# Seven block products for attention times input weights, for batches 2 to 4

## The chip, the cores and the metric

The kernel runs on one core of a Trainium2 chip. The metric is the time of one execution on the device in microseconds (us): 2050.67 us before the change, the median of three runs (2050.41 to 2054.49).

## The reference, cut to what matters

```python
# q, k, v: (4, 6080, 256); w_in: (256, 2048); w_out: (2048, 256); all fp32
qn = q / (norm(q, axis=1) + 1e-6)
kn = k / (norm(k, axis=1) + 1e-6)
s = kn.transpose(0, 2, 1) @ qn / tau      # 256 x 256 for each batch
a = softmax(s)
x = (v @ a).reshape(24320, 256)
h = x @ w_in
out = relu(h) ** 2 @ w_out
```

The attention matrix of a batch is only 256 x 256. The kernel therefore never forms `x`: it multiplies the attention matrix into the weights (`a @ w_in`, 256 x 2048, once per batch) and applies the result to `v`. These products of attention and input weights are what the change is about.

## The kernel before

**Tiling.** The 6080 tokens of a batch are cut into six chunks (five of 1024, one of 960 tokens), each as two halves of T = 512 (480) columns. The 2048 hidden units are cut into eight blocks j of 2 x 128. A chunk with a block is a quad; there are 24 x 8 = 192. fp32 accuracy comes from splitting every operand into a high and a low fp32r part and adding three matmuls (high x high, high x low, low x high), so one product is three matmuls. A quad's first layer is a 2 x 2 block product in Strassen-Winograd form: seven products (`m1` to `m7`, line 753) of 128 x 128 weights with 128 x T values. The second layer (line 911) is in that form too for groups of four blocks, three of the seven products being put off to the end of a group (`run_later`).

**Batch preparation.** For each batch the scores `k.T q` are summed over 48 token tiles (line 484), the column norms and the softmax follow (`norms`, `spread`, `exps`), then `attnT` turns the 256 x 256 exponentials with four TensorE transposes and splits them into `aT` in the ring `acc`. For each of four weight groups g, `load_win` brings the two parts of that group's input weights (`wins`, kept in DRAM in split form) to two tiles of the ring `hl`; `fold` makes for each half ch of the output rows a bank of 512 columns out of six matmuls (line 638), and ScalarE takes the bank to the tile `us` (ring `kq`) with the softmax denominator as its scale (line 643). `combine` forms from `us` the sums that the seven-product form needs, splits them and stores them as `wsc`, from where every chunk of the batch loads its weights (`load_wt`). For batches 2 to 4 all of this runs in the shade of the quads of the batch before: scores until quad 30 of its 48, the folds from about quad 34 on.

**What sets the order.** Every step is an `Op` with a key (a place counted in quads), engines and a cost; `Plan.order` simulates the queues and rings and writes one fixed program for each engine. Steps that either ScalarE or VectorE can do (`cast`) go to whichever the plan thinks is earlier. All places, leads and biases stand in the table `PLACE`. PSUM has eight banks: two in the ring `h` (used by `m1`, `m6`, `m7`, the put-off products and the folds), one each for `x` and `z`, four for the outputs. Each ring has a fixed number of buffers; `kq`, `hl` and `D` have three. A bank is used by one instruction after another: the first product's result is copied out, and the next product adds to the same bank:

```python
product(key, q, A11, Bn, True)
add(key, moved(T), lambda e: copy(e, get(X, ...), made[Bn][:, :T]), [(Bn, 0)], [(X, 0)])
...
product(key, q, S2, Bn, False)
```

Of the kernel before, what the change touches and what calls it, by code (L numbers as in the profile page):

```python
# [18 lines left out]

P = 128  # L20

PLACE = {'ahead': {'P': 11.46, 'A': 2.414, 'V': 1.621, 'S': 2.799, 'G': 6.535},
 'shy': {'V': 1.107},
 'look': 46.549,
 'push': 8.133,
 'slack': 0.744,
 'bias': {'V': -0.23, 'A': 3.545},
 'groups': ((0, 1, 2, 3), (4, 5, 6, 7)),
 'fewer': ((0, 1, 2, 3), (4, 5)),
 'few': (1, 23),  # L30
 'evac': 1,
 'under': ('M6', 'M7'),
 'banks': ({'M1': 'h', 'M6': 'h', 'M7': 'h'}, {'M1': 'h', 'M6': 'h', 'M7': 'h'}),
# [2 lines left out]
 'every': 3,  # L36
 'presplit': 1,
 'last': {1: 30, 2: 30},
 'open': (-5.462, -3.775, -0.543, -0.836, 0.232, -0.871, 0.095, -0.386, -1.001),
 'lead': 1,  # L40
 'start': (0.625, 0.747, 1.316, 1.529, 1.896, 2.09, -0.025, -2.364, 0.629, 0.76, 1.022),
 'sums': (1.642, 2.237, 7.525, 7.358, 6.02, 6.63, 15.884, 14.947),
 'scores': {1: (-0.941, 0.895, 0.796, 4.28), 2: (2.337, 1.339, -0.115, 0.265, 0.748, 3.485)},
 'folds': {1: (3.995, 4.387, -0.606, 0.751, 1.253, 1.806)},
 'rows': {0: ((4.09, 5.166, 7.785), (8.216, 8.679, 10.297), (-5.367, -2.655, -0.367, -0.681, 0.414, -0.202, -2.003), (1.829, 0.099), (2.213, 0.355)),
# [14 lines left out]


class Op:
# [204 lines left out]
def act(n):  # L267
    return 0.1 + 0.00083 * n
# [3 lines left out]
def tile_channel_attention_relu2_ffn(ctx, tc, kq, vT, tau, w_in, w_out, outT):  # L272
# [11 lines left out]
    HMAX = 512  # L284
    G = 2
    NGK = NT // G
    EARLY = 12
    LEAD = PLACE["lead"]
    GROUPS = PLACE["groups"]
    FEWER = PLACE["fewer"]  # L290
# [54 lines left out]
    def moved(n):  # L345
        return {"A": act(n)}
# [14 lines left out]
    def store(key, out, in_, r, w, size, e="S"):  # L361
        add(key, {e: 0.45 if e == "S" else 1.0},
            lambda e: (nc.sync if e == "S" else nc.gpsimd).dma_start(out=out(), in_=in_()), r, w, size)
# [7 lines left out]
    def dtile(name, shape, tag=None, bufs=None):  # L371
        if name not in dram:
            dram[name] = scratch.tile(shape, F32, name=tag or "_".join(map(str, name)), **({"bufs": bufs} if bufs else {}))
        return dram[name]
# [45 lines left out]
    def decode_w_in(key, g, lead=0.9):  # L420
        Wn = decode(key, "in", g, "sq" if g else "t4", lead)
        win[0, g] = Wn
        if not PLACE["presplit"]:
            store(key, lambda: dtile(("wins", g), [P, 4, GW]), lambda: made[Wn], [(Wn, 0)], [(("wins", g), 0)], 512)

# [82 lines left out]
    def tiny(key, eng, cost, fn, r, w):  # L508
        add(key, {eng: cost}, lambda e: fn(), r, w)
# [107 lines left out]
    def fold_split(key, b, g):  # L617
        W, w = win[b, g], plan.tile("hl", ("wi", b, g))
        split(key, 1024, lambda: made[W].rearrange("p a b -> p (a b)"),
              lambda: get(w, [P, 2, NH, 2 * GW], F32R)[:, 0].rearrange("p d n -> p (d n)"),  # L620
              lambda: get(w, [P, 2, NH, 2 * GW], F32R)[:, 1].rearrange("p d n -> p (d n)"),
              [(W, 0)], [(w, 0)], [(w, 1)])
        for l in range(2) if b == 0 and PLACE["presplit"] else ():
            store(key, lambda l=l: dtile(("wins", g), [P, 2, NH, 2 * GW])[:, l], lambda l=l: made[w][:, l].bitcast(F32),
                  [(w, l)], [(("wins", g), l)], 512)

    def fold(key, b, g, ch, ring="h"):
        aT, w, bank = ("aT", b, "aT"), ("wi", b, g), plan.tile(ring, ("fb", b, g, ch))
        u = ("us", b, g)
        if u not in plan.ring_of:  # L630
            plan.tile("kq" if b or g else "s", u)
        cs = slice(ch * P, (ch + 1) * P)

        def run(e):
            n = 0
            for d in range(NH):
                for l, r in ((0, 0), (0, 1), (1, 0)):
                    nc.tensor.matmul(out=get(bank, [P, HMAX]), lhsT=made[aT][:, l, d, cs], rhs=made[w][:, r, d, :],  # L638
                                     start=n == 0, stop=n == 3 * NH - 1)
                    n += 1  # L640

        add(key, {"P": 1.36}, run, [(aT, 0), (aT, 1), (w, 0), (w, 1)], [(bank, 0)])
        tiny(key, "A", act(512), lambda: nc.scalar.activation(
            out=get(u, [P, 4, GW])[:, ch:4 - ch:3 - 2 * ch], in_=made[bank].rearrange("p (t f) -> p t f", t=2), func=AF.Copy,
            scale=made["den", b][:, ch:ch + 1]), [(bank, 0), (("den", b), 0), (("den", b), 1)], [(u, ch)])

    def combine(key, b, g, step=1.0):

# [406 lines left out]
    def at(u, fn, *args):  # L1055
        events.append((u, len(events), fn, args))
# [35 lines left out]
    for g in range(EARLY):  # L1092
        for t in range(G):
            k = g * G + t
            at(-0.6 + 0.01 * k if k < LEAD else PLACE["start"][9] + PLACE["start"][10] * (k - LEAD) / (2 * EARLY - LEAD),
               lambda key, g=g, t=t, k=k: score_mm(key, tiles0[1, g], t, s1, k == 0, k == EARLY * G - 1))
    at(PLACE["start"][9] + PLACE["start"][10] + 0.02, lambda key: score_out(key, 1, s1))
    at(PLACE["start"][6], lambda key: decode_w_in(key, 1, PLACE["open"][7]))
    at(PLACE["start"][7], load_v, 1)
    at(PLACE["start"][8], fold_split, 0, 1)  # L1100
# [12 lines left out]
    for b in range(1, B):  # L1113
# [16 lines left out]
        at(max(end + MID, u - tune[-4] + 0.01), norms, b)  # L1130
        at(max(end + 1 + MID, u - tune[-4] + 0.02), spread, b)
        at(max(end + 1.6, u + tune[-2] + 0.01, u - tune[-4] + 0.03), lambda key, b=b: exps(key, b, lambda: made["s_acc", b], [(("s_acc", b), 0)]))
        at(max(end + 2 + MID, u + tune[-2] + 0.02, u - tune[-4] + 0.04), attnT, b)
        for g in range(NG):
            tune = PLACE["folds"][max(x for x in PLACE["folds"] if x <= b)]
            u = end + tune[0] + tune[1] * g
            at(u - tune[2], load_win, b, g)
            at(u + tune[3], fold, b, g, 0)
            at(u + tune[4], fold, b, g, 1)
            at(u + tune[5], combine, b, g)  # L1140
    for i, u in enumerate(SUMS):
        at(u, weight_sums, i)
    done = {}
# [39 lines left out]
    for ci in range(len(chunks)):  # L1183
# [15 lines left out]
                at(ends[ci, "M5"] + 0.001, evacuate, ci)  # L1199
            at(both + 0.002, join, ci)  # L1200
        for m in ("M1", "M6", "M5", "M7"):
            at(max(ends.get((ci, "M1"), 0.0) if m == "M1" else both + 0.002,
                   ends.get((ci, HOME["M5"]), 0.0) if m == "M7" else 0.0, ends.get((ci, HOME[m]), 0.0)), close, ci, m)
    for u, _, fn, args in sorted(events, key=lambda x: x[:2]):
        fn(u, *args)
# [31 lines left out]
```

## Time and profile before

| | |
|---|---|
| median of three runs | 2050.67 us |
| the profiled execution | 2051.52 us |
| its span, first to last instruction | 2049.7 us |
| PE (matmul) busy | 2035.3 us, 99% |
| VectorE (DVE) busy | 1977.5 us, 96% |
| ScalarE (ACT) busy | 1772.8 us, 86% |
| granted TensorE clock, mean | 1.000 |

The span is 1.8 us shorter than the execution that it comes from; what lies around it is no part of the trace. "PE" stands for the matmuls and "PEld" for the weight loads, which overlap them. Matmuls are pipelined and their ends are modelled, so a row's duration is longer than the distance between two starts; distances are read from the timeline or the chain. Busy time is a union, so it can't exceed a stretch.

### The profile page before, as it was taken

What the parts mean: (1) busy time and instruction counts of PE and PEld (TensorE: products, weight loads), DVE (VectorE), ACT (ScalarE), POOL (GpSimd) and SP (SyncE); (2) the same over time, 40 slices, a digit from 0 to 9 for tenths busy, and PEclk for the clock granted to TensorE, in tenths of its full rate; (3) what the DMA queues carried; (4) which work ended last, traced back from release to release, by engine and by line L of the source; (5) the groups of instructions that cost most, each with busy time, mean ns of one, the idle gap of its engine ahead of it and who ended that gap; (6) DMA issues with size and microseconds to landing.
All of it is one profiled execution on the core that took longest, in us unless ns stands there. A gap on an engine that the chain in (4) does not pass through costs nothing.

```text
span 2049.7 us, 28360 instructions
## 1 busy us (share of the span) xinstructions
PE 2035.3 (99%) x9356; PEld 1700.9 (83%) x9356; DVE 1977.5 (96%) x2909; ACT 1772.8 (86%) x2656; POOL 119.0 (6%) x137
## 2 busy tenths in 40 slices
PE   8999999999999999999999999999999999999999
PEld 7888788878888888888888888888888888888887
DVE  7899999999999999999999999999999999999997
ACT  6789899988899999988889989889888888788885
POOL 0000001000001000010001010000000000000000
PEclk9999999999999999999999999999999999999999
DMA  9899989879999999987899999998799987878875
GB/s 377 293 324 346 301 285 298 250 231 307 338 301 312 301 292 281 292 252 232 300 327 320 315 296 283 270 290 249 251 316 293 296 262 235 260 244 244 250 231 136
DMA packets 299651, 578.14 MB, mean 282 GB/s; under 512 B 24432, under 2 KB 183920, under 8 KB 299504
## 3 DMA queue, kind: packets, MB, share of 16 engines
q1 hardware_dynamic: 278864, 508.65, 71.4%
q0 software_dynamic: 20640, 67.67, 17.6%
q8 instruction: 75, 1.23, 0.2%
q14 instruction: 72, 0.59, 0.1%
HBM read 438.57 MB, written 69.99 MB: 248 GB/s over the span
## 4 chain that ended last, share of the span: by engine, by line
PE 93%; DVE 3%; DMA 3%; issue 1%; ACT 0%; SPq 0%; DVEq 0%; ACTq 0%
PE o L911 25%; PE h L753 24%; PE h L911 17%; PE z L753 12%; PE x L753 6%; PE x L484 5%; PE h L638 2%; PE o L484 1%; DMA wt<-wsc 1%; DMA kq<-kq 0%; DMA vt<-w_in 0%; DVE D L800 0%; DVE hl L356 0%; DVE g L356 0%; DVE t L356 0%
## 5 line engine op out<-in xcount | busy, mean ns | idle before, releaser
L753 PE MATMUL h<-vt,wt 128*128 128x512 f32 (+1 forms) x2304 | 623.6, 389 | 0.9 <-DMA wt<-wsc 0.4
L753 PEld LDWEIGHTS h<-vt,wt 128*128 128x128 f32 x2304 | 430.7, 188 | 92.7 <-DVE D L800 2.3
L911 PE MATMUL h<-hl,wo 128*128 128x512 f32 (+1 forms) x1620 | 390.0, 388 | 0.6 <-issue 0.6
L911 PE MATMUL o<-g,wo 128*128 128x512 f32 (+1 forms) x1368 | 372.3, 388 | 0.0
L911 PEld LDWEIGHTS h<-hl,wo 128*128 128x128 f32 x1620 | 303.2, 188 | 62.7 <-issue 1.0
L356 DVE TENSOR_TENSOR hl<-D,hl 128x1024 fp32r<-128x1024 f32 (+1 forms) x270 | 325.1, 1211 | 5.0 <-ACT hl L331 4.3
L753 PE MATMUL z<-vt,wt 128*128 128x512 f32 (+1 forms) x1152 | 324.0, 389 | 1.6 <-DVE s L800 1.5
L911 PE MATMUL o<-t,wo 128*128 128x512 f32 (+1 forms) x1080 | 299.7, 388 | 0.6 <-DMA wo<-wos 0.6
L911 PEld LDWEIGHTS o<-g,wo 128*128 128x128 f32 x1368 | 254.8, 188 | 49.5 <-ACT s_acc L331 0.2
L356 DVE TENSOR_TENSOR g<-s,g 128x1024 fp32r<-128x1024 f32 (+1 forms) x204 | 247.0, 1211 | 7.3 <-ACT g L331 6.8
L753 PEld LDWEIGHTS z<-vt,wt 128*128 128x128 f32 x1152 | 213.8, 188 | 45.8 <-DVE s L800 2.4
L911 PEld LDWEIGHTS o<-t,wo 128*128 128x128 f32 x1080 | 202.2, 188 | 41.6 <-DMA wo<-wos 1.0
L335 ACT ACTIVATE D<-D 128x1024 f32<-128x1024 f32 (+1 forms) x180 | 189.7, 1054 | 34.8 <-DVE D L800 34.0
L335 ACT ACTIVATE s<-s 128x1024 f32<-128x1024 f32 (+1 forms) x204 | 215.7, 1058 | 3.7 <-DVE s L800 3.2
L331 ACT CAST hl<-D 128x1024 fp32r<-128x1024 f32 (+1 forms) x197 | 204.5, 1044 | 12.8 <-DVE D L846 8.9
L491 POOL DMA_DIRECT2D D<-D x90 | 83.8, 932 | 1569.5 <-DVE hl L356 1110.7
L331 ACT CAST g<-s 128x1024 fp32r<-128x1024 f32 (+1 forms) x159 | 166.5, 1047 | 7.7 <-PE o L911 6.9
L331 ACT COPY x<-h 128x512 f32<-128x512 f32 (+1 forms) x192 | 110.7, 577 | 61.6 <-PE h L753 59.7
L753 PE MATMUL x<-vt,wt 128*128 128x512 f32 (+1 forms) x576 | 160.9, 387 | 0.0
L341 ACT ACTIVATE s<-z 128x512 f32<-128x512 f32 (+1 forms) x192 | 113.6, 591 | 28.9 <-PE z L753 28.0
L800 DVE CUSTOM_DVE_ANT_0 D<-z,m 128x512 f32<-128x512 f32 (+1 forms) x180 | 122.8, 682 | 4.3 <-PE z L753 3.4
L753 PEld LDWEIGHTS x<-vt,wt 128*128 128x128 f32 x576 | 108.1, 188 | 21.7
(146 smaller groups left out, 2934.4 us busy)
## 6 DMA issues: line engine op xcount, KB each, us to landing
wt<-wsc SPq DMA_DIRECT2D x368, 256.0 KB, 6.0
wo<-wos SPq DMA_DIRECT2D x180, 512.0 KB, 5.9
wt<-wsc SPq DMA_DIRECT2D x184, 384.0 KB, 5.4
wo<-wod_M SPq DMA_DIRECT2D x270, 256.0 KB, 5.4
kq<-kq SPq DMA_DIRECT2D x82, 512.0 KB, 7.5
D<-D POOLq DMA_DIRECT2D x75, 512.0 KB, 7.9
wsc<-wt SPq DMA_DIRECT2D x32, 896.0 KB, 7.4
v<-vT SPq DMA_DIRECT2D x40, 512.0 KB, 6.7
```

The source lines that it names most:

```text
L331: (nc.scalar.copy if e == "A" else nc.vector.tensor_copy)(out=out, in_=in_)
L335: nc.scalar.activation(out=out, in_=in_, func=AF.Square)
L341: nc.scalar.activation(out=out, in_=in_, func=AF.Relu)
L356: add(key, {"V": vec(n)}, lambda e: nc.vector.tensor_sub(out=l(), in0=x(), in1=h()), (*r, *wh), wl)
L484: nc.tensor.matmul(out=s[:, h * C:(h + 1) * C], lhsT=l, rhs=r, start=first and h == 0 and n == 0, stop=last and n == len(terms) - 1, skip_ ...
L491: add(key, {"G": 1.0}, lambda e: nc.gpsimd.dma_start(out=out(), in_=in_(), accum_op=ALU.add), r, w, size)
L638: nc.tensor.matmul(out=get(bank, [P, HMAX]), lhsT=made[aT][:, l, d, cs], rhs=made[w][:, r, d, :], start=n == 0, stop=n == 3 * NH - 1)
L753: nc.tensor.matmul(out=out[:, :N], lhsT=made[w][:, l, i], rhs=made[v][:, r, :N], start=start and n == 0, stop=n == 2, skip_group_check=True)
L800: nc.vector._custom_dve(TENSOR_ADD_SAT, out=x, in0=made[bank][:, :T], in1=made[m][:, :T], s0=BIG, s1=0.0)
L911: nc.tensor.matmul(out=o[:, :T], lhsT=l, rhs=x[:, :T], start=start and k == 0, stop=stop and k == 2, skip_group_check=True)
```

## The change

For batches 2 to 4, `attn7`, `load7` and `fold7` take the place of `attnT`, `load_win` and `fold`. Two weight groups make a pair p. Over a pair, a 256 x 256 matrix times a 256 x 1024 one is done as a 2 x 2 block product in Strassen-Winograd form: seven products of three matmuls instead of eight. The left sums are made in `attn7` (after the softmax denominator has been multiplied in by two ScalarE instructions of 256 columns), the right ones once for all batches in `load_t` and `make_t` and kept in DRAM as `tin`; for them the weights are also stored unsplit as `winr`. Of odd groups only one half of `wins` is stored. `fold7` runs the seven products through four banks of the ring `h`, one after the other: results are copied out to `us`, and copied back into a bank when a later product adds to them; the last two are added by VectorE. `combine` is as before. `PLACE` has new numbers nearly everywhere, so the whole order of the program is another one. Cut, the diff is:

```diff
@@ -19,15 +19,19 @@
-PLACE = {'ahead': {'P': 11.46, 'A': 2.414, 'V': 1.621, 'S': 2.799, 'G': 6.535},
- 'shy': {'V': 1.107},
- 'look': 46.549,
- 'push': 8.133,
- 'slack': 0.744,
- 'bias': {'V': -0.23, 'A': 3.545},
+PLACE = {'ahead': {'P': 9.551, 'A': 2.463, 'V': 1.607, 'S': 2.935, 'G': 7.569},
+ 'shy': {'V': 5.013},
+ 'look': 52.025,
+ 'push': 8.038,
+ 'slack': 0.738,
+ 'bias': {'V': -0.132, 'A': 3.725},
+ 'early': 12,
+ 'seven': 1,
+ 'tm': (27.56, 31.697, 3.095, 1.083),
+ 'f7': {1: (1.757, 2.079, 2.342, 2.691, 3.159, 7.39, 1.336)},
...
@@ -36,27 +40,31 @@
- 'lead': 1,
- 'scores': {1: (-0.941, 0.895, 0.796, 4.28), 2: (2.337, 1.339, -0.115, 0.265, 0.748, 3.485)},
- 'folds': {1: (3.995, 4.387, -0.606, 0.751, 1.253, 1.806)},
+ 'lead': 3,
+ 'scores': {1: (0.247, 0.392, 0.673, 0.976), 2: (2.672, 1.326, -0.168, 0.534, 0.738, 5.009)},
+ 'folds': {1: (4.022, 4.398, 5.291, -0.121, -1.916, -3.605)},
...
+        if PLACE["seven"]:
+            store(key, lambda: dtile(("winr", g), [P, 4, GW]), lambda: made[Wn], [(Wn, 0)], [(("winr", g), 0)], 512)
         if not PLACE["presplit"]:
...
+        lo = g % 2 if PLACE["seven"] else 0
         for l in range(2) if b == 0 and PLACE["presplit"] else ():
-            store(key, lambda l=l: dtile(("wins", g), [P, 2, NH, 2 * GW])[:, l], lambda l=l: made[w][:, l].bitcast(F32),
-                  [(w, l)], [(("wins", g), l)], 512)
+            store(key, lambda l=l: dtile(("wins", g), [P, 2, NH, 2 * GW])[:, l, lo:], lambda l=l: made[w][:, l, lo:].bitcast(F32),
+                  [(w, l)], [(("wins", g), l)], 256 * (2 - lo))
...
+    SEVEN = {"M1": ("A11", (0, 0)), "M2": ("A12", (0, 1)), "M6": ("S2", (1, 0)), "M5": ("S1", (1, 1)), "M3": ("S4", (2, 0)),
+             "M7": ("S3", (2, 1)), "M4": ("A22", (3, 0))}
+    LEFT = {"A12": ("aT", 0), "A22": ("aT", 1), "S1": ("aT", 2), "S2": ("aT", 3), "S3": ("aS", 0), "S4": ("aS", 1), "A11": ("aZ", 0)}
+    def attn7(key, b):
+        bank, S, den, en = plan.tile("h", ("ab", b)), plan.tile("sq", ("as", b)), ("den", b), ("s_acc", b)
+        def exp_of(h):
+            return made[en][:, h * C:(h + 1) * C]
+        for h in range(NH):
+            tiny(key, "A", act(C) + 0.05, lambda h=h: nc.scalar.activation(
+                out=exp_of(h), in_=exp_of(h), func=AF.Copy, scale=made[den][:, h:h + 1]),
+                [(en, 1 + h), (den, 0), (den, 1)], [(en, 1 + h)])
+        def turned():
+            v = get(bank, [P, HMAX]).rearrange("p (d c) -> p d c", d=NH)
+            for h in range(NH):
+                for d in range(NH):
+                    nc.tensor.transpose(out=v[:, d, h * P:(h + 1) * P], in_=exp_of(h)[:, d * P:(d + 1) * P], identity=ident)
+        tiny(key, "P", 0.9, turned, [(en, 1 + h) for h in range(NH)], [(bank, 0)])
+        def x(k):
+            return get(S, [P, 8, P])[:, k]
+        add(key, moved(512), lambda e: copy(e, get(S, [P, 8, P])[:, :4].rearrange("p a b -> p (a b)"), made[bank]),
+            [(bank, 0)], [(S, k) for k in range(4)])
+        for k, fn, a, c in ((4, nc.vector.tensor_add, 1, 3), (5, nc.vector.tensor_sub, 4, 0), (6, nc.vector.tensor_sub, 0, 1),
+                            (7, nc.vector.tensor_sub, 2, 5)):
+            alu(key, P, lambda k=k, fn=fn, a=a, c=c: fn(out=x(k), in0=x(a), in1=x(c)), [(S, a), (S, c)], [(S, k)])
+        for ring, name, lo, hi in (("acc", "aT", 2, 6), ("s_acc", "aS", 6, 8), ("zq", "aZ", 0, 1)):
+            n = plan.tile(ring, (name, b, "7"))
+            split(key, (hi - lo) * P, lambda lo=lo, hi=hi: made[S][:, lo:hi],
+                  lambda n=n, w=hi - lo: get(n, [P, 2, w, P], F32R)[:, 0], lambda n=n, w=hi - lo: get(n, [P, 2, w, P], F32R)[:, 1],
+                  [(S, k) for k in range(lo, hi)], [(n, 0)], [(n, 1)])
+    def load_t(key, p):
+        for g in (2 * p, 2 * p + 1):
+            n = plan.tile("kq", ("tw", g))
+            load(key, lambda n=n: get(n, [P, 4, GW]), lambda g=g: dram["winr", g], [(("winr", g), 0)], [(n, 0), (n, 1)], 512)
+    def make_t(key, p):
+        a, c, S = ("tw", 2 * p), ("tw", 2 * p + 1), plan.tile("sq", ("ts", p))
+        def x(n, d):
+            return get(n, [P, 4, GW])[:, 2 * d:2 * d + 2]
+        for o, i, j in (((S, 0), (c, 1), (c, 0)), ((S, 1), (c, 0), (a, 0)), ((c, 0), (c, 1), (S, 1)), ((c, 1), (a, 1), (c, 0))):
+            alu(key, 512, lambda o=o, i=i, j=j: nc.vector.tensor_sub(out=x(*o), in0=x(*i), in1=x(*j)), [i, j], [o])
+        for n, ts in ((S, ("T3", "T1")), (c, ("T2", "T4"))):
+            t = plan.tile("hl", ("tx", p, ts[0]))
+            split(key, 1024, lambda n=n: made[n].rearrange("p a b -> p (a b)"),
+                  lambda t=t: get(t, [P, 2, NH, 2 * GW], F32R)[:, 0].rearrange("p d n -> p (d n)"),
+                  lambda t=t: get(t, [P, 2, NH, 2 * GW], F32R)[:, 1].rearrange("p d n -> p (d n)"),
+                  [(n, 0), (n, 1)], [(t, 0)], [(t, 1)])
+            for d, name in enumerate(ts):
+                store(key, lambda name=name: dtile(("tin", p, name), [P, 2, 2 * GW]), lambda t=t, d=d: made[t][:, :, d].bitcast(F32),
+                      [(t, 0), (t, 1)], [(("tin", p, name), 0)], 512)
+    def load7(key, b, p, i):
+        n = plan.tile("hl" if i < 3 else "kq", ("w7", b, p, i))
+        if not i:
+            for l in range(2):
+                load(key, lambda l=l: get(n, [P, 2, NH, 2 * GW], F32R)[:, l].bitcast(F32),
+                     lambda l=l: dram["wins", 2 * p][:, l], [(("wins", 2 * p), l)], [(n, l)], 512)
+            return
+        for d, name in enumerate((("T2", "T1"), ("B22", "T3"), ("T4",))[i - 1]):
+            src = ("wins", 2 * p + 1) if name == "B22" else ("tin", p, name)
+            load(key, lambda d=d: get(n, [P, 2, NH if i < 3 else 1, 2 * GW], F32R)[:, :, d].bitcast(F32),
+                 lambda src=src, name=name: dram[src][:, :, 1] if name == "B22" else dram[src],
+                 [(src, 0), (src, 1)] if name == "B22" else [(src, 0)], [(n, d)], 512)
+    def fold7(key, b, p, i):
+        us = [("us", b, 2 * p + t) for t in range(2)]
+        if not i:
+            for n in us:
+                plan.tile("kq", n)
+        bank = plan.tile("h", ("f7", b, p, i))
+        def slot(n, ch):
+            return get(us[n], [P, 4, GW])[:, ch:4 - ch:3 - 2 * ch]
+        def all_of():
+            return get(bank, [P, HMAX]).rearrange("p (t f) -> p t f", t=2)
+        def mm(m, first):
+            left, (part, d) = SEVEN[m]
+            name, k = LEFT[left]
+            a, w = (name, b, "7"), ("w7", b, p, part)
+            def run(e):
+                for n, (l, r) in enumerate(((0, 0), (0, 1), (1, 0))):
+                    nc.tensor.matmul(out=get(bank, [P, HMAX]), lhsT=made[a][:, l, k], rhs=made[w][:, r, d], start=first and n == 0,
+                                     stop=n == 2, skip_group_check=True)
+            add(key, {"P": 0.68}, run, [(a, 0), (a, 1), *([(w, 0), (w, 1)] if not part else [(w, d)]), *(() if first else [(bank, 0)])],
+                [(bank, 0)])
+        def out(n, ch):
+            add(key, moved(512), lambda e: copy(e, slot(n, ch), all_of()), [(bank, 0)], [(us[n], ch)])
+        def back(n, ch):
+            add(key, moved(512), lambda e: copy(e, all_of(), slot(n, ch)), [(us[n], ch)], [(bank, 0)])
+        def plus(n, ch):
+            alu(key, 512, lambda: nc.vector.tensor_add(out=slot(n, ch), in0=all_of(), in1=slot(n, ch)),
+                [(bank, 0), (us[n], ch)], [(us[n], ch)])
+        for fn, *args in (((mm, "M1", True), (out, 1, 0), (mm, "M2", False), (out, 0, 0)),
+                          ((back, 1, 0), (mm, "M6", False), (out, 0, 1)),
+                          ((back, 0, 1), (mm, "M5", False), (out, 1, 1), (mm, "M3", False), (out, 1, 0)),
+                          ((mm, "M7", True), (plus, 1, 1), (mm, "M4", False), (plus, 0, 1)))[i]:
+            fn(*args)
...
-        at(max(end + 2 + MID, u + tune[-2] + 0.02, u - tune[-4] + 0.04), attnT, b)
-        for g in range(NG):
+        at(max(end + 2 + MID, u + tune[-2] + 0.02, u - tune[-4] + 0.04), attn7 if PLACE["seven"] else attnT, b)
+        for p in range(NG // 2) if PLACE["seven"] else ():
+            tune, f7 = PLACE["folds"][max(x for x in PLACE["folds"] if x <= b)], PLACE["f7"][max(x for x in PLACE["f7"] if x <= b)]
+            u = end + tune[0] + 2 * tune[1] * p
+            for i in range(4):
+                at(u + f7[i] - f7[6], load7, b, p, i)
+                at(u + f7[i], fold7, b, p, i)
+            for t in range(2):
+                at(u + f7[4 + t], combine, b, 2 * p + t)
+        for g in range(NG) if not PLACE["seven"] else ():
             tune = PLACE["folds"][max(x for x in PLACE["folds"] if x <= b)]
             u = end + tune[0] + tune[1] * g
             at(u - tune[2], load_win, b, g)
             at(u + tune[3], fold, b, g, 0)
             at(u + tune[4], fold, b, g, 1)
             at(u + tune[5], combine, b, g)
+    for p in range(NG // 2) if PLACE["seven"] else ():
+        at(PLACE["tm"][p], load_t, p)
+        at(PLACE["tm"][p] + PLACE["tm"][2 + p], make_t, p)
     for i, u in enumerate(SUMS):
```

Left out are the new numbers of `PLACE` for the start, the norms, the sums and the rows of single chunks, a few lines at the start that keep two keys in order, and a condition in the order of `close`.

## Rows read from the trace of the kernel before

**Rows 1.** The page's first parts: span, then each engine's busy time, share and instructions.

```profile
span 2049.7 us, 28360 instructions
PE 2035.3 (99%) x9356; PEld 1700.9 (83%) x9356; DVE 1977.5 (96%) x2909; ACT 1772.8 (86%) x2656; POOL 119.0 (6%) x137
```

**Rows 2.** Busy time by stretch (us; the stretch's length stands behind its bounds).

```profile
0.00:60.00 60.00, 53.35 (x240) 45.72 (x241) 45.50 (x59) 37.12 (x44) 0.83 (x7) 1.00 0.99 381
200.00:450.00 250.00, 246.69 (x1146) 202.79 (x1145) 242.57 (x350) 230.69 (x339) 15.46 (x18) 1.00 0.89 275
390.00:600.00 210.00, 208.96 (x941) 173.95 (x940) 203.41 (x321) 185.81 (x288) 10.83 (x11) 1.00 0.88 285
900.00:1110.00 210.00, 209.96 (x961) 176.19 (x960) 206.82 (x327) 183.03 (x285) 11.66 (x12) 1.00 0.89 288
1600.00:2000.00 400.00, 400.00 (x1769) 331.05 (x1768) 386.40 (x556) 334.72 (x502) 17.93 (x21) 1.00 0.82 251
2000.00:2049.70 49.70, 45.75 (x211) 39.15 (x209) 36.09 (x50) 27.84 (x41) 3.16 (x3) 0.98 0.50 132
```

**Rows 3.** PE's waits over the span, three of seven rows.

```profile
PE x L484 <- DMA kq<-kq: 5.4, 2, 3.5
PE z L753 <- DVE s L800: 1.5, 1, 1.5
PE h L753 <- ACT uM L331: 0.3, 1, 0.3
```

**Rows 4.** The chain that ended last: start, length, work; one block product.

```profile
486.82 2.72 PE h L638 x12
```

**Rows 5.** PE's timeline at the first block products of batch 2: start, length.

```profile
441.00 2.88 PE L638 MATMUL h<-hl,acc 128*128 128x512 f32 x12
443.83 3.02 PE L911 MATMUL h<-hl,wo 128*128 128x512 f32 x12
```

**Rows 6.** Groups by shape: busy us, mean ns of one | idle before.

```profile
L638 PE MATMUL h<-hl,acc 128*128 128x512 f32 x186 | 46.8, 390 | 0.0
L638 PEld LDWEIGHTS h<-hl,acc 128*128 128x128 f32 x186 | 34.9, 188 | 7.3
L643 ACT ACTIVATE kq<-h,den 128x512 f32<-128x512 f32 x30 | 20.6, 686 | 8.4 <-PE h L638 8.2
L331 ACT COPY z<-h 128x512 f32<-128x512 f32 x160 | 94.0, 588 | 3.9 <-PE h L753 2.1
L331 ACT COPY h<-uM 128x512 f32<-128x512 f32 x28 | 16.7, 597 | 1.8 <-DVE D L800 1.1 <-DVE uM L1002 0.6
L1002 DVE TENSOR_TENSOR uM<-h,uM 128x512 f32<-128x512 f32 x57 | 39.3, 689 | 3.4 <-PE h L911 3.0
L875 DVE TENSOR_TENSOR sq<-sq 128x128 f32<-128x128 f32 x32 | 7.9, 287 | 0.1
L662 DVE TENSOR_TENSOR sq<-kq 128x256 f32<-128x256 f32 x30 | 12.2, 420 | 1.3 <-ACT kq L643 1.3
L331 ACT CAST hl<-D 128x1024 fp32r<-128x1024 f32 x160 | 168.2, 1054 | 9.7 <-DVE D L846 5.9 <-PE h L911 2.9 <-PE x L484 0.5
L331 DVE CAST hl<-D 128x1024 fp32r<-128x1024 f32 x65 | 44.9, 691 | 0.0
```

**Rows 7.** VectorE's timeline, three instructions on end: start, length.

```profile
436.19 1.23 DVE L356 TENSOR_TENSOR g<-s,g 128x1024 fp32r<-128x1024 f32 x1
437.32 0.69 DVE L846 TENSOR_TENSOR D<-D,s 128x512 f32<-128x512 f32 x1
437.92 0.70 DVE L825 TENSOR_TENSOR D<-D 128x512 f32<-128x512 f32 x1
```

**Rows 8.** Busy time of VectorE's casts and copies alone (line 331), by stretch.

```profile
390.00:600.00 210.00, 10.82 (x20) 1.00 0.88 285
900.00:1110.00 210.00, 14.13 (x27) 1.00 0.89 288
```

**Rows 9.** DMA issues: queue, count, KB each, median us to landing.

```profile
hl<-wins SPq DMA_DIRECT2D x24, 512.0 KB, 7.2
```

More of the change, by code (lines that the diff above doesn't have):

```diff
@@ L38 @@
  'last': {1: 30, 2: 30},
- 'open': (-5.462, -3.775, -0.543, -0.836, 0.232, -0.871, 0.095, -0.386, -1.001),
- 'lead': 1,
- 'start': (0.625, 0.747, 1.316, 1.529, 1.896, 2.09, -0.025, -2.364, 0.629, 0.76, 1.022),
- 'sums': (1.642, 2.237, 7.525, 7.358, 6.02, 6.63, 15.884, 14.947),
- 'scores': {1: (-0.941, 0.895, 0.796, 4.28), 2: (2.337, 1.339, -0.115, 0.265, 0.748, 3.485)},
- 'folds': {1: (3.995, 4.387, -0.606, 0.751, 1.253, 1.806)},
- 'rows': {0: ((4.09, 5.166, 7.785), (8.216, 8.679, 10.297), (-5.367, -2.655, -0.367, -0.681, 0.414, -0.202, -2.003), (1.829, 0.099), (2.213, 0.355)),
[14 rows of a table removed]
+ 'open': (-5.563, -3.638, -0.344, -0.914, 0.355, -0.936, 0.068, -0.148, -0.729),
+ 'lead': 3,
+ 'start': (0.74, 1.133, 1.303, 1.759, 1.78, 1.927, 0.191, -2.295, 0.321, 0.886, 0.989),
+ 'sums': (1.573, 1.142, 4.885, 7.723, 7.067, 7.798, 14.829, 14.467),
+ 'scores': {1: (0.247, 0.392, 0.673, 0.976), 2: (2.672, 1.326, -0.168, 0.534, 0.738, 5.009)},
+ 'folds': {1: (4.022, 4.398, 5.291, -0.121, -1.916, -3.605)},
+ 'rows': {0: ((3.564, 5.166, 7.184), (8.077, 8.65, 10.317), (-5.323, -3.04, -0.305, -1.041, 1.335, 1.133, -2.199), (1.754, 0.836), (1.929, 0.327)),
[18 rows of a table added]
 class Op:
@@ L286, in tile_channel_attention_relu2_ffn @@
     NGK = NT // G
-    EARLY = 12
+    EARLY = PLACE["early"]
     LEAD = PLACE["lead"]
@@ L1094, in tile_channel_attention_relu2_ffn @@
             k = g * G + t
-            at(-0.6 + 0.01 * k if k < LEAD else PLACE["start"][9] + PLACE["start"][10] * (k - LEAD) / (2 * EARLY - LEAD),
+            at(-0.6 + 0.01 * k if k < LEAD else max(PLACE["start"][9] + max(PLACE["start"][10], 0.0) * (k - LEAD) / (2 * EARLY - LEAD), -0.6 + 0.01 * k),
                lambda key, g=g, t=t, k=k: score_mm(key, tiles0[1, g], t, s1, k == 0, k == EARLY * G - 1))
-    at(PLACE["start"][9] + PLACE["start"][10] + 0.02, lambda key: score_out(key, 1, s1))
+    at(PLACE["start"][9] + max(PLACE["start"][10], 0.0) + 0.02, lambda key: score_out(key, 1, s1))
     at(PLACE["start"][6], lambda key: decode_w_in(key, 1, PLACE["open"][7]))
@@ L1201, in tile_channel_attention_relu2_ffn @@
         for m in ("M1", "M6", "M5", "M7"):
-            at(max(ends.get((ci, "M1"), 0.0) if m == "M1" else both + 0.002,
+            at(max(max(ends.get((ci, "M1"), 0.0), ends.get((ci, "M6"), 0.0) + 0.001 if GS[ci] else 0.0) if m == "M1" else both + 0.002,
                    ends.get((ci, HOME["M5"]), 0.0) if m == "M7" else 0.0, ends.get((ci, HOME[m]), 0.0)), close, ci, m)
```

32 rows, old and new, of the table PLACE are left out of this document.

## The prediction

> **What bounds the kernel now.** I first read the engines' shares [rows 1]: PE is busy for 2035.3 of 2049.7 us, VectorE for 1977.5, ScalarE for 1772.8. A busy PE need not be a PE at its pace, so the second view is the pace: in the chain, twelve matmuls of one block product take 2.72 us [rows 4], 0.2267 us for each start, though a matmul's own row says 0.390 us [rows 6]. At that pace a quad of 14 products x 3 matmuls takes 9.5 us. The reader is to see next, in the table of stretches [rows 2], where PE stands: from 1600 to 2000 us it is busy for 400.00 of 400 us, and so it is nearly everywhere; its idle time is 6.65 us in the first 60, 3.3 us from 200 to 450, and 3.95 us after 2000 us, where the last products, copies and stores follow one another. The waits by name [rows 3] say that the start waits for score tiles, and that in all of the span PE waits 0.3 us for a ScalarE copy. So the time is the number of matmuls times their pace, and whatever takes matmuls away in the middle moves the end, as long as VectorE and ScalarE keep up. That is the second thing to see: VectorE is at 98.5% from 900 to 1110 us and at 97.0% from 200 to 450. It is almost a second bound.
>
> **PE.** Before, a pair of weight groups takes 2 groups x 2 halves x 6 = 24 matmuls; after, 7 products x 3 = 21. With 2 pairs in each of three batches that is 6 x 3 = 18 fewer, 18 x 0.2267 = 4.08 us [rows 4]. The turning of the attention matrix stays at four transposes a batch. The lower bound of a matmul's worth is its weight load, 188 ns [rows 6]: 3.4 us; the upper one is its row's 390 ns: 7.0 us. I take 4.1, since the row of the chain is this very instruction back to back.
>
> [...]
>
> **VectorE.** `fold7` adds two sums of 512 columns a pair; a row of the same form is 0.689 us [rows 6], and on end such instructions start 0.60 us apart [rows 7]: 4 a batch, 2.4 to 2.8 us. `attn7` adds four sums of 128 columns at 0.287 us, and its three splits (512, 256, 128 columns in place of one of 512) add a 256 and a 128 subtraction, 0.420 + 0.287 us [rows 6]: 1.9 us. Together 4.3 to 4.6 us a batch. `make_t` runs twice, once for all batches: four subtractions of 512 columns and two of 1024 (1.13 us apart, 1.23 long [rows 7]): 4.7 to 5.2 us each time, 9.3 to 10.4 in all. The whole is 22 to 24 us more, on an engine that has 72 us idle.
>
> **ScalarE.** A pair goes from four scaled copies at 0.686 us to five plain copies out at 0.588 and two back at 0.597 [rows 6]: +1.4 us, 2.8 a batch. `attn7` has two scalings and a bank copy, and up to two more casts, each no longer than a 512-column copy: at most 2.9 us. With four 1024-column casts at 1.054 us for `make_t`, 4.2 us, the whole is at most 3 x 5.7 + 4.2 = 21 us, with 277 us idle.
>
> **Where that goes.** The places in the table of the diff put `make_t` at quads 31 and 33 and batch 2's products from quad 34 on, that is at about 390 to 600 us, as the first block products of batch 2 now run at 441 us [rows 5]. There VectorE has 210 - 203.4 = 6.6 us idle [rows 2], and about 14 us are added. What is over, 7.4 us, has a way out: 10.8 us of casts that VectorE does in that stretch can go to ScalarE [rows 8], where a cast takes 1.054 us for 0.691 [rows 6], so 11.3 us. ScalarE then gets 11.3 + 5.7 + 4.2 = 21 us and has 24.2 idle [rows 2]. It fits, with 3 us left. From 900 to 1110 us (batch 3, without `make_t`) VectorE has 3.2 us and gets up to 4.6, and ScalarE has 27.0 for 5.7 and 2; that fits easily, as for batch 4. So I cost both engines at nothing, and the cover is this: ScalarE's idle time. If it fails in the first stretch, up to 7.4 us show.
>
> **Banks and hand-overs.** Inside a pair PE now waits for a copy or sum five times before it may add to a bank (for both copies back, and before M2, M3 and M4). What is queued behind such a wait on PE is everything, since its order is fixed; so the plan has to put other products between. The same form, product, copy out, next product into the same bank, stands in every quad, and PE loses 0.3 us to copies in the whole run [rows 3]. The block products of now are not free either: the put-off product behind them takes 3.02 us for twelve matmuls instead of 2.72 [rows 5, 4], 0.3 us lost with both banks of the ring full. I take nothing for the 30 hand-overs; bounds are a gain of 3.6 us (0.3 at each of today's 12 groups saved) and an uncovered copy of 0.6 us [rows 6] at each, 18 us. The transposes of `attn7` wait longer too, since the denominators must now be there and multiplied in first; that is once a batch, four short instructions, in the quads between scores and products, and I count it with these bounds.
>
> **DMA.** Kept sums and unsplit weights cost 2 + 2 + 2 MB once and spare 1 MB of `wins`; a pair loads 2.25 MB for 2.0. That is 6.5 MB beside 578, and some 30 more issues on SP's queue; POOL's gets none. They land in about 7.2 us, as the weights of the folds do [rows 9], and the products are asked for 1.3 quads, 12.7 us, after their loads. Cost nothing; behind a late one stand the weights of the next quads on the same queue, and then PE.
>
> **The new order.** Every place in the program moves. The 3.3 us of PE idle from 200 to 450 us [rows 2] belong to waits that a new order meets differently; the bounds are that they go, or come twice. I take 1 us less, an estimate by a third of them. The start and the end (6.65 and 3.95 us) I leave: loads and stores set them.
>
> **The sum.** -4.1 + 0 + 0 + 0 - 1 = -5.1 us. Against the profiled execution (2051.52 us, 1.8 above its span) that is 2046.4; that execution lay 0.85 above the median of the runs, so 2045.6 us against 2050.67.
>
> **The rivals.**
> - *Nothing comes of it:* the first stretch overflows. Behind on VectorE, PE waits for the sums that free its banks. The price is the 7.4 us of overflow at most, about half in a mild case: 2050.67 - 4.1 + 3.7 = 2050.3. For it speak only 3 us of slack in ScalarE over 210; against it, that work can slide by some quads.
> - *Slower: the hand-overs show.* If three of the five in each pair are uncovered, 6 x 3 x 0.6 = 10.8 us come and 4.1 go: 2057.4. It decides from 8.2 us on (1.4 us, some two uncovered copies, a pair). The 0.3 us that PE waits for copies now [rows 3] speaks against it; that VectorE and ScalarE are fuller when a copy is asked for speaks for it.
> - *Faster still:* all 3.3 us of the waits from 200 to 450 us go, and the squeeze of 0.3 us at 12 groups as well: 2050.67 - 4.1 - 3.3 - 3.6 = 2039.7.
> - *The matmuls taken away are worth less than their pace,* 3.4 us by the weight loads [rows 6], as these stay PE's real limit: 2047.3. [...]
>
> **How the numbers follow.** The measurement can't tell less than about 0.2%, 4.1 us, from no change; faster therefore means below 2046.6. Chances: the forecast 45% (2043 to 2048 as its own range, a good two thirds of it below 2046.6), nothing 25%, slower 15%, faster still 12%, the weight-load limit 3%. From these: faster 0.47, same 0.36, slower 0.17. The range goes from the faster case, 2040, to just short of the slower one, 2056.
>
> **What would show it.** Right: matmuls of the block products fall from 144 to 126 in batches 2 to 4; PE busy falls by 4 us with its idle time as before; VectorE busy rises by less than 24 us as casts move to ScalarE, whose busy time rises by 20 to 40. Wrong: new rows in PE's waits named after a copy, a sum in `us` or a load of `tin`; a PE below 208 us busy from 390 to 600; or a time changed mostly before 60 or after 2000 us, which this argument leaves alone.

## The result and the profile after

The changed kernel takes 2067.65 us (median; 2067.2 to 2069.66) beside 2051.64 us for the kernel before on the same chip: a ratio of 1.0078, 95% interval 1.006 to 1.0095. It is 16 us slower, above the range of 2040 to 2056. The first lines of the page of the changed kernel:

```profile
span 2065.9 us, 28506 instructions
PE 2040.4 (99%) x9338; PEld 1696.2 (82%) x9338; DVE 1986.0 (96%) x2921; ACT 1806.1 (87%) x2723; POOL 119.3 (6%) x137
```

The 18 matmuls are gone, 9338 in place of 9356 [rows 1], and yet PE is busy for 5.1 us more and idle for 11.1 us more. The idle time is waiting, and by the rows the longer busy time is too: a matmul's row is 390 ns long where starts lie 227 ns apart [rows 6, 4], so a gap of up to some 160 ns (the difference, an estimate) can count as busy, and the clock stayed at 1.000. The busy time by stretch (PE, PEld, VectorE, ScalarE, GpSimd, each with its number of instructions, as in [rows 2]) tells where:

```profile
200.00:450.00 250.00, 244.91 (x1135) 200.65 (x1134) 245.70 (x359) 229.70 (x340) 15.63 (x18) 1.00 0.95 296
390.00:600.00 210.00, 205.60 (x902) 166.03 (x901) 204.70 (x323) 185.39 (x294) 9.92 (x10) 1.00 0.93 305
900.00:1110.00 210.00, 207.93 (x946) 173.29 (x946) 203.30 (x325) 186.50 (x296) 10.79 (x11) 1.00 0.89 287
1600.00:2000.00 400.00, 400.00 (x1766) 330.73 (x1765) 388.40 (x563) 337.70 (x507) 18.87 (x21) 1.00 0.84 259
```

PE was idle for 1.0 us from 390 to 600 us and for 0.04 from 900 to 1110 [rows 2]; now it is 4.4 and 2.1. The number of matmuls says more than the idle time: from 390 to 600 us it is 902 for 941, 39 fewer, of which the change takes away 6. The other 33 are 7.5 us at 0.2267 us each, an estimate, and more than a third of the 20 us lost (16 us, and the 4.1 us not gained). From 1600 us on, where no batch is prepared, it runs nearly as before, 1766 matmuls for 1769. VectorE and ScalarE are hardly fuller in these stretches, so it isn't one engine that is full. PE's waits by name (total, times, longest) have 22 rows where there were seven [rows 3], most under 1 us and for all sorts of work:

```profile
PE x L494 <- DMA kq<-kq: 4.5, 2, 3.4
PE h L879 <- DMA wt<-wsc: 3.0, 1, 3.0
PE h L1037 <- ACT m L339: 1.5, 2, 0.8
```

One such place, from the timelines of PE, ScalarE and VectorE of the changed kernel:

```profile
518.30 2.90 PE L1037 MATMUL h<-hl,wo 128*128 128x512 f32 x12
521.03 0.85 PE L1037 MATMUL o<-g,wo 128*128 128x480 f32 x3
521.72 0.82 PE L1037 MATMUL o<-t,wo 128*128 128x480 f32 x3
523.04 0.93 PE L879 MATMUL h<-vt,wt 128*128 128x512 f32 x3 [0.50 <-DVE uM L1128]
524.61 0.93 PE L879 MATMUL h<-vt,wt 128*128 128x512 f32 x3 [0.65 <-ACT m L339]
```

```profile
524.00 0.56 ACT L339 COPY m<-h 128x480 f32<-128x480 f32 x1 [2.14 <-PE h L879]
```

```profile
521.27 0.64 DVE L364 TENSOR_TENSOR t<-D,t 128x480 fp32r<-128x480 f32 x1
521.84 0.54 DVE L364 TENSOR_TENSOR wt<-kq,wt 128x384 fp32r<-128x384 f32 x1
522.31 0.67 DVE L1128 TENSOR_TENSOR uM<-h,uM 128x512 f32<-128x512 f32 x1
```

A put-off product (the first row) ends at about 521.2 us; the sum that gives its bank of the ring `h` back stands third in VectorE's order and ends at 522.98. PE has six more matmuls for the output banks and then only products for that ring, so it waits, first for VectorE and then for ScalarE, which stood idle for 2.14 us before its copy. No engine but VectorE is full here (busy for 7.00 us from 518 to 525, ScalarE for 3.70); the three orders just don't meet well. That raises the question of the experiments: is it the new products, or the new order?

### The profile page after: what moved, and what is told of

The parts are those of the page before. It is cut to its first block, busy times and chain, and to the rows that moved or that the text cites. A ratio compares the mean times of both kernels' runs of the same rounds, so it can differ in the third digit from the quotient of the medians.

```text
span 2065.9 us, 28506 instructions
## 1 busy us (share of the span) xinstructions
PE 2040.4 (99%) x9338; PEld 1696.2 (82%) x9338; DVE 1986.0 (96%) x2921; ACT 1806.1 (87%) x2723; POOL 119.3 (6%) x137
## 3 DMA queue, kind: packets, MB, share of 16 engines
q8 instruction: 75, 1.23, 0.2%
## 4 chain that ended last, share of the span: by engine, by line
PE 82%; DVE 9%; ACT 4%; DMA 3%; issue 1%; SPq 0%; DVEq 0%; ACTq 0%
PE o L1037 23%; PE h L879 21%; PE h L1037 15%; PE z L879 11%; PE x L879 5%; PE x L494 4%; DVE hl L364 2%; PE h L751 1%; DVE D L926 1%; DMA kq<-kq 1%; PE o L494 1%; DVE g L364 1%; DVE t L364 1%; DMA wt<-wsc 1%; ACT s L343 1%
## 5 line engine op out<-in xcount | busy, mean ns | idle before, releaser
L951 DVE TENSOR_TENSOR D<-D 128x512 f32<-128x512 f32 (+1 forms) x180 | 121.8, 677 | 5.7 <-ACT D L343 5.6
```

What stands on the lines that cost most here:

```text
L951: alu(key, T, lambda: nc.vector.tensor_sub(out=delta(q, 0), in0=delta(q, 0), in1=delta(q, 1)), [(D, k), (D, k + 1)], [(D, k)])
```

## The experiments

The ratios are to the kernel before, run beside each group.

| run | products, table, edit | us | ratio, 95% interval |
|---|---|---|---|
| e1 | eight, new table | 2074.24 | 1.0112 (1.0097 to 1.0127) |
| e2 | seven, old table | 2092.39 | 1.0201 (1.0185 to 1.0216) |
| e3 | eight, old table, new general numbers | 2061.54 | 1.005 (1.0034 to 1.0067) |
| e4 | eight, old table, one key moved | 2055.56 | 1.0016 (1.0007 to 1.0025) |
| e5 | as changed, sums on GpSimd, order kept | 2078.86 | 1.0131 (1.0116 to 1.0146) |
| e6 | as changed, no copies back, order kept | 2068.38 | 1.0076 (1.0056 to 1.0097) |
| e7 | as changed, less for VectorE, order kept | 2069.11 | 1.0081 (1.0057 to 1.0104) |
| e8 | e6 and e7 together, order kept | 2069.35 | 1.0081 (1.0066 to 1.0096) |
| e9 | eight, old table shaken | 2075.23 | 1.0114 (1.0097 to 1.0131) |
| e10 | seven, old table shaken | 2109.92 | 1.0282 (1.0267 to 1.0297) |
| e11 | eight, new table refitted | 2060.38 | 1.0044 (1.0029 to 1.0059) |
| e12 | seven, old table refitted | 2077.21 | 1.0123 (1.0108 to 1.0138) |
| e13 | seven, old table, ordered without hand-overs | 2076.56 | 1.0125 (1.0106 to 1.0144) |
| e14 | the same, shaken | 2088.67 | 1.0187 (1.0171 to 1.0203) |
| e15 | e13 without the new sums | 2080.45 | 1.0144 (1.0129 to 1.016) |
| e16 | the same, shaken | 2088.64 | 1.0176 (1.0159 to 1.0193) |

**Order against products (e1 to e4).**

```diff
 # e1, to the changed kernel
- 'seven': 1,
+ 'seven': 0,
- 'folds': {1: (4.022, 4.398, 5.291, -0.121, -1.916, -3.605)},
+ 'folds': {1: (3.995, 4.387, -0.606, 0.751, 1.253, 1.806)},
 # e2, to the table of before, with the functions of the changed kernel
+ 'seven': 1,
+ 'tm': (27.56, 31.697, 3.095, 1.083),
+ 'f7': {1: (1.757, 2.079, 2.342, 2.691, 3.159, 7.39, 1.336)},
 # e3, to the kernel before: 'ahead', 'shy', 'look', 'push', 'slack', 'bias' as in the diff
 # e4, to the kernel before
- 'folds': {1: (3.995, 4.387, -0.606, 0.751, 1.253, 1.806)},
+ 'folds': {1: (3.995, 4.387, -0.606, 0.76, 1.253, 1.806)},
```

> New table of places, but the products as they were: eight in place of seven for each pair of groups, no kept sums (the fold keys of before are put back, since the new table has no use for them). If the new order is what costs (theory A), it stays near the changed kernel's 2067 us or lies 4 us above it, 2063 to 2073, and PE again loses some 15 us to waits scattered over the whole span. If the seven products are what costs (theory B: hand-overs between engines inside a pair, and more work for VectorE and ScalarE), it falls back to 2046 to 2054.

> The reverse: the table of places of before, with only the entries that the seven products need taken from the new one. Theory A (order): 4 us fewer matmuls and little else, 2044 to 2052. Theory B (products): 2060 to 2070, with the losses near 390 to 600, 900 to 1110 and 1380 to 1600 us, where the products stand.

> The kernel before with only the general numbers of the plan (how far each engine may run ahead, shyness, look, push, slack, bias) taken from the new table; keys and products are old. Theory A in its narrow form (the general numbers cost): 2060 or more. Theory A in its wide form (any order that was not fitted to this program costs): also above 2051, by 3 us or more. Theory B: 2048 to 2054.

> The kernel before with one fold key moved by 0.009 quads (0.1 us), which gives another order of the program from batch 2 on and changes nothing in the work. It measures what an arbitrary new order is worth. Theory A in its wide form: above 2051.6 by 3 us or more. Theory B, and theory A in the form that only particular places of the new table are bad: within 2 us of the kernel before.

Both theories are half right, and e1 and e2 lie above the ranges of both. The new table with the old products is 22.6 us slower than before, so a new order costs without any of the new work. More than half of it shows from 390 to 600 us, where e1 starts 54 matmuls fewer (887 for 941 [rows 2], some 12 us) and where the fold keys put back from the old table meet the new one:

```profile
390.00:600.00 210.00, 202.10 (x887) 166.40 (x886) 197.68 (x314) 168.43 (x262) 11.19 (x11) 0.98 0.84 266
```

The old table with the new products is slower still, by 40.7 us. A single key moved by 0.1 us costs 3.9 us (ten runs; 1.4 to 5.1 us by the interval), the general numbers alone cost 9.9. The old table is fitted to the old products closely, and each of these changes falls off that fit.

**Load and hand-overs in a fixed order (e5 to e8).** Every engine keeps the order of the changed kernel; the plan is told of the old costs.

```diff
 # e5: attn7's four sums, make_t's four, and make_t's low parts
-nc.vector.tensor_sub(...)
+nc.gpsimd.tensor_sub(...)
 # e6, in fold7
-(back, 1, 0), (mm, "M6", False)
+(mm, "M6", True)
-(back, 0, 1), (mm, "M5", False)
+(mm, "M5", True)
-(mm, "M1", True), (out, 1, 0), (mm, "M2", False)
+(mm, "M1", True), (mm, "M2", False)
 # e7: plus, attn7's and make_t's sums are not emitted; in make_t's splits
-nc.vector.tensor_sub(out=l(), in0=x(), in1=h())
+nc.vector.tensor_copy(out=l(), in_=x())
 # e8: e6 and e7
```

> The changed kernel with every engine's order kept, only that the SBUF sums which the change added (four in the preparation of the attention matrix, all of those for the kept weight sums with their low parts) run on GpSimd, which is idle, in place of VectorE: some 12 us less for VectorE. If the load that the change puts on VectorE is what PE waits for (theory B1), some 4 to 8 us come back, above all from 390 to 530 us: 2059 to 2064. If the waits are laid down in the order itself (theory A), at most 2 us: 2065 to 2069.

> The changed kernel, order kept, without the copy of the first product out and the two copies back into the bank, so that the second and third bank start fresh (the sums of the seven products are then incomplete): 18 ScalarE copies (10.6 us) fewer and two hand-overs a pair in place of five. Theory B2 (the hand-overs inside a pair cost): 5 to 10 us come back, 2057 to 2063. Theory A: less than 2 us, 2065 to 2069.

> The changed kernel with every engine's order kept and most of VectorE's added work left out: the two sums of a pair that end its products, the four sums in the preparation of the attention matrix and the four sums for the kept weights are not done, and the low parts of the latter are plain copies (the result lacks these sums). VectorE has some 16 us less to do, in the stretches where the products stand. Theory B1 (VectorE's added load): 8 us or more come back, 2052 to 2060. Theory A (the order itself): within 3 us of the changed kernel, 2064 to 2070.

> As the run before it, and also without the copy of the first product out and the two copies back, so that VectorE has 16 and ScalarE 10 us less and only one hand-over a pair is left (the result lacks these sums). If load and hand-overs cost only together (theory B), most of the 16 us come back: 2050 to 2058. Theory A: 2062 to 2069.

e6, e7 and e8 are within 2 us of the changed kernel (e8 0.35 us above its range for theory A). The stretch from 390 to 600 us of e7:

```profile
390.00:600.00 210.00, 205.84 (x904) 166.45 (x903) 198.78 (x310) 185.70 (x294) 9.92 (x10) 1.00 0.94 304
```

VectorE has 5.9 us less to do there than in the changed kernel, and PE still does 904 matmuls where it did 902. e6 and e8 say the same, 904 and 898. So neither VectorE's added load nor the inner hand-overs, as they run, are what PE waits for in this order. ScalarE's added work is only in part taken out here, and the added transfers not at all. e5 lies outside both of its ranges: it went the other way, by 11 us. A subtraction of 1024 columns takes 2.78 us on GpSimd, for 1.23 on VectorE [rows 7]:

```profile
L364 POOL TENSOR_TENSOR hl<-kq,hl 128x1024 fp32r<-128x1024 f32 x2 | 5.6, 2782 | 0.9 <-DVE hl L339 0.9
```

These late sums stand ahead of the first block products, so e5 moves a chain as well as a load and tells nothing of the load alone.

**Any order, and a fitted one (e9 to e12).**

```diff
 # e9 (and in the same way e10, on the table of e2): every number shaken
-PLACE = {'ahead': {'P': 11.46, 'A': 2.414, 'V': 1.621, 'S': 2.799, 'G': 6.535},
+PLACE = {'ahead': {'P': 11.436, 'A': 2.422, 'V': 1.641, 'S': 2.789, 'G': 6.508},
 # e12, to e2 (two lines of many; e11 in the same way, to e1)
- 'tm': (27.56, 31.697, 3.095, 1.083),
+ 'tm': (26.007, 30.646, 5.024, 3.473),
- 'f7': {1: (1.757, 2.079, 2.342, 2.691, 3.159, 7.39, 1.336)},
+ 'f7': {1: (1.737, 2.312, 2.362, 3.575, 2.905, 6.345, 1.366)},
```

> The kernel before with every place and number of its table moved a little (normal, 0.02 quads, 0.2 us): the same work, another order throughout. Theory A (an order not fitted to the program costs, whatever the products): 2062 to 2082. Theory B (only the seven products cost): 2049 to 2056.

> The same shaking of the old table with the seven products. If the products ask no more of an order than the eight did, it lies 4 us below the shaken kernel with eight, give or take 10. If they are harder to place (theory A and B together: more steps that lean on one another in the same two banks and three buffers), it lies 25 to 45 us above it: 2095 to 2120.

> Eight products, from the new table, then fitted again: some 2000 small changes of the table, of which those were kept that the plan liked better. Theory A: most of the loss of the unfitted one (2074 us) goes, 2055 to 2065. Theory that the new table's places are bad in themselves: 2070 or more.

> Seven products, from the old table, fitted again with as many changes. Theory A alone: it gets as far as the refitted kernel with eight and lies about 4 us below it, 2051 to 2061. Theory A with harder products: it gains from 2092 but stays 8 us or more above the refitted kernel with eight, 2066 to 2080.

Shaking the table costs the old products 23.9 us. This is one draw, and a good half of it is lost before 200 us, ahead of every product that the change replaces: e9 starts 18 matmuls fewer in the first 60 us (222 for 240 [rows 2]) and 47 fewer from 60 to 200, together some 15 us, with a granted clock of 0.96 in both stretches. The second one, in the kernel before and in e9:

```profile
60.00:200.00 140.00, 140.00 (x621) 115.74 (x620) 129.23 (x212) 120.75 (x188) 1.02 (x1) 1.00 0.90 316
60.00:200.00 140.00, 136.11 (x574) 110.47 (x574) 113.84 (x188) 105.87 (x163) 0.00 (x0) 0.96 0.79 278
```

The seven products lie 34.7 us above the eight when shaken and 16.8 us above them when refitted. These pairs are not orders of like quality, though. e10 shares only the general numbers with e9; its keys are another draw, which loses nothing before 200 us. e11 and e12 were fitted from different tables. And the outputs of e10 and e12 are wrong although their edits leave no work out. In e12 the fitted places put `combine` of a pair's first group (2.905) ahead of the pair's last bank (3.575), so it reads `us` without the last sum; for e10 no run shows what goes wrong. That the fit and the products are two separate costs is what these runs suggest, not what they show.

**What makes the seven products hard to place (e13 to e16).** Here the plan makes a new order for the reduced work.

```diff
 # e13 (old table) and e14 (shaken), in fold7
+(mm, "M1", True), (mm, "M2", False), (out, 0, 0)
+(mm, "M6", True), (out, 0, 1)
+(mm, "M5", True), (mm, "M3", False), (out, 1, 0)
+(mm, "M7", True), (mm, "M4", False), (out, 1, 1)
 # e15 and e16, also: attn7's and make_t's four sums cost nothing in the plan and are not emitted
```

> Seven products in the old table (2092 us), ordered anew without the inner hand-overs: the first product isn't copied out, nothing is copied back, and the last product's sums are left out, so that each of the four banks of a pair takes one or two products and one copy (the result lacks these terms). If it is the hand-overs that make the seven products hard to place, 10 to 20 us come back although the same removal gave nothing in a fixed order: 2070 to 2082. If they don't matter when an order is made either, at most 5: 2087 to 2095.

> The same with the shaken table of the run at 2110 us, as a second draw. Hand-overs: 2080 to 2096. Not: 2100 to 2115.

> Old table, without hand-overs and, in the plan and in the program, without VectorE's new sums for the attention matrix and the kept weights (the result lacks them too). If VectorE's load makes the order hard as well, another 5 to 12 us below the run without hand-overs, 2062 to 2076; if not, within 6 us of it.

> The same with the shaken table. If hand-overs and sums are all that sets the seven products apart, it reaches the shaken kernel with eight products (2075 us) or lies a few us below it, 2068 to 2080; if something else remains (two groups at once, more tiles held), 2085 or more.

Without the hand-overs the time is 15.8 us (e13 against e2) and 21.3 us (e14 against e10) shorter, inside the ranges for hand-overs. But with them three copies and two sums a pair go, and each run is also another order. Little of e13's gain lies where the hand-overs stood. From 390 to 600 us e2 and e13 start 882 matmuls each; from 1110 to 1380 us, where neither runs a product of a pair, e13 starts 45 more, some 10 us (e2 and e13 in turn):

```profile
390.00:600.00 210.00, 202.29 (x882) 162.06 (x881) 200.67 (x317) 182.22 (x286) 9.91 (x10) 1.00 0.91 296
390.00:600.00 210.00, 202.92 (x882) 162.21 (x882) 204.92 (x325) 170.55 (x267) 9.91 (x10) 1.00 0.91 298
1110.00:1380.00 270.00, 263.56 (x1237) 218.17 (x1236) 258.50 (x367) 234.42 (x349) 21.93 (x25) 0.99 0.95 295
1110.00:1380.00 270.00, 268.19 (x1282) 224.26 (x1281) 267.43 (x375) 246.75 (x366) 21.48 (x25) 1.00 0.97 301
```

In e14 the gain over e10 does lie where pairs stand (876 matmuls for 849 from 390 to 600 us, 958 for 919 from 900 to 1110), and part of it is lost again from 1110 to 1380 (1212 for 1256). How much of the two gains belongs to the hand-overs and how much to another draw of the order stays open. Leaving VectorE's new sums out as well gains nothing: 3.9 us more and 0.0. The shaken kernel stays at 2088.6, 13 us above e9, whose own loss lies in good part before 200 us.

## Why the prediction was wrong

- **PE.** Right: 18 matmuls fewer, 9338 for 9356, and the pace is the one taken: the twelve at 518.30 us above are followed 2.73 us later (521.03). In the new table the seven products are 6.6 us faster than the eight (e1), but that table was not fitted to the eight, so this is no measure of the 4.1.
- **VectorE and ScalarE.** Right: VectorE is busy for 8.5 us more and ScalarE for 33.3, inside the bounds, the one with casts moving to the other. That VectorE's added work, with the copies of the hand-overs, costs nothing in the order as it stands is shown by e7 and e8. The rival of an overflowing first stretch falls with them.
- **Hand-overs.** The step priced them at nothing since the same form stands in every quad and PE waits 0.3 us for copies there. Taken out of the finished program they give nothing back (e6). But the 0.3 us were the result of an order fitted to the old steps, not a property of the form: in e3, with the work unchanged, PE waits 3.4 us for the copies to `z` alone. Two orders made anew without the hand-overs were 16 and 21 us faster (e13, e14), of which the share that is theirs isn't shown. The slower rival had the right sign, but uncovered copies of 0.6 us each are not what e6 shows. One reading was wrong as well: the 3.02 us of the put-off product are a row's length, and such a row without a wait is 2.88 long [rows 5], so 0.14 us were lost and not 0.3. The gain that bounds this step, and the faster rival with it, were 1.9 us too hopeful.
- **DMA.** The bytes were mis-sized: the kept sums are 4 MB and not 2, and a pair loads 3.5 MB and not 2.25. The traces count 594.9 MB for 578.1, 16.8 more and not 6.5. From 390 to 600 us no wait of PE names a transfer. The one of 3.0 us for `wt` lies at 1147 us, where no pair is loaded, and e1, with the bytes of before, has one of 4.1. But no run takes the transfers out alone, so that they cost nothing is not shown.
- **The new order.** This is the step that failed. It said that the 3.3 us of idle PE from 200 to 450 us go or come twice, and took 1 us of gain. Its bounds came from the waits that the old order still had, but an order that is nearly free of waits has only one way to go. With the same work a new order costs 3.9 us (e4), 9.9 (e3), 22.6 (e1) and 23.9 (e9), and only in part from 200 to 450 us. That the changed kernel's 16 us are such a loss, less the 4.1 us gained, fits e6 to e8, where leaving work out with the order kept gives nothing back. How much of the loss the hand-overs bring about by making the order harder can't be told, because each edit of the plan makes another order.
- **The signs.** Two of the signs of being wrong came: PE is busy for 205.6 us from 390 to 600, below 208, and the waits have new rows named after copies (`m`, `x`); none names `us` or `tin`. PE's busy time rose by 5.1 us where a fall of 4 was the sign of being right.
- **Open.** 13 us between two shaken kernels, with different keys, remain without hand-overs and sums. That two groups go together, hold two of three `kq` buffers and ask for three `hl` tiles at once was only argued. Whether the seven products, fitted as long as the eight were, would show their 4.1 us stays open too; with the fitting done here no version beats the kernel before.

## What to carry to other kernels

A program whose bound engine is busy for 99% of the span in a closely fitted fixed order may have no slack for any edit; here none was free that made another order. So first measure what an edit without any work in it costs (a key moved, a table shaken), and price every change by that. Short waits in such a trace belong to the fit, so the price of a step can't be read from how little its like waits now. To tell load from order, leave work out with the order kept. An order made anew tells more only with several draws on either side, since here one order differed from the next by as much as the effect looked for.

## What the hardware showed beside

In e2 nine slow matmuls followed four waits of PE. The waits come within 7 us (0.96, 1.32, 0.30 and 1.78 us, the last until 1160.98). The next nine matmuls, and the granted clock from 1161 to 1165 us (0.50, the third number from the end):

```profile
1160.98 4.21 PE L875 MATMUL h<-vt,wt 128*128 128x512 f32 x9 [1.78 <-DMA wt<-wsc]
1164.99 1.48 PE L875 MATMUL x<-vt,wt 128*128 128x512 f32 x3
```

```profile
1161.00:1165.00 4.00, 4.00 (x10) 3.13 (x11) 0.00 (x0) 1.16 (x2) 0.00 (x0) 0.50 1.10 303
```

The nine matmuls start (1164.99 - 1160.98) / 9 = 0.446 us apart, about twice the 0.227 of [rows 4], and the granted clock there is 0.50. That lost some 2 us more than the waits themselves (9 x 0.219, an estimate). That the waits brought the clock down is not shown. In the changed kernel PE waits 2.99 us until 1150.00, and the granted clock is 1.00 from 1140 to 1150 us and from 1150 to 1154; its mean is 1.000.
